# Attention, soft MoE and maxout on one core: loading q and k as pairs of tokens

## The chip, the cores and the metric

The kernel runs on one core of a Trainium2 chip. Five engines work side by side: TensorE (PE, with its weight loads as PEld), VectorE (DVE), ScalarE (ACT), GpSimd (POOL) and SyncE (SP), which issues the DMAs. The metric is the device time of one execution in microseconds.

## The reference

Three stages follow one another, all in float32:

```
scores = scale * q_c @ k_c^T          # 64-token chunks, 8 batches x 8 heads, 9 chunks, head size 64
attn = exp(scores - max) ; attn /= sum + 1e-9
out = attn @ v_c                      # -> x [4608, 512]

logits = x @ phi                      # soft MoE: 8 experts x 4 slots
slot_input = softmax over tokens(logits)^T @ x
h = relu(slot_input[e] @ w1[e]) ; slot_out[e] = h @ w2[e]
x = softmax over slots(logits) @ slot_out

h = max(x @ w1, x @ w2, x @ w3)       # maxout, 512 -> 768 -> 512
y = h @ w_out                         # these four weights arrive as float64
```

## The kernel before

The 4608 tokens are cut into 18 units of 256 tokens; an **item** is one unit and four of the eight heads, so there are 36 items, 0 to 35. The kernel has three stages: the attention loop over items (which also computes the logits, the running softmax over tokens and the slot sums, and decodes the float64 maxout weights to float32), the eight experts, and the maxout with the output.

The loop is pipelined by hand. In iteration i each name in `ORDER` emits one step for its item, and the instructions of every engine run in the order in which they were emitted. The steps that the change and the prediction touch, with their lines before the change:

- `ld` (L431 to L443): the loads on SP's queue: q and k of item i+3 (`load_qk`, L153), V (`load_v`, L144), one piece of float64 weight `r` (`load_raw`, L409), and now and then a 1 MB chunk `w` of expert weights (`load_chunk`, L114), of which `NPRE` = 13 are loaded inside the loop into memory that the attention does not use. 32 chunks are needed in all; the others are loaded as the attention's memory comes free, from line 572 on, and then as the experts use up the ring.
- `Tk`, `Tq` (L171): transposes of raw k and q of item i+1 on PE; `ke`, `qe` (L182, L178): their copies from PSUM to SBUF on ACT.
- `S` (L193): 32 matmul records of 64x64 scores of item i; `mx`, `sub` (L203, L208) on DVE; `exp` (L214) on ACT in the next iteration.
- `PT` (L222), `PTe` (L227), `PV` (L240): transpose of the exponentials, copy, product with V for item i-1.
- `rd`, `rec`, `nrm` (L250, L254, L260): normalisation on DVE for item i-2; `XT`, `XTe` (L275, L280): transpose of its result.
- `da` on ACT (L416), `d0`, `d1`, `d2` on DVE (L421, L423, L427): decoding of one piece `r`, in iterations 1 to 31; pieces have 256 columns (18) or 384 (12).
- every fourth iteration: `st` (L307 to L313, statistics of the logits), `ex` and `ss`, `eT`, `sm` and `sa` (L351 and L360, slot sums), `l0` and `l1` (L297).

A raw q or k tile has two buffers, `r` two, V two. One tile of q or k is loaded with tokens on the partitions: every token of a head is one 256-byte piece in memory (64 floats), 1024 such pieces for q and as many for k and for V in an iteration.

Of the kernel before, what the change touches and what calls it, by code (L numbers as in the profile page):

```python
# [8 lines left out]
F32 = mybir.dt.float32  # L9
# [3 lines left out]
ALU = mybir.AluOpType  # L13
# [5 lines left out]
def kernel(  # L19
# [32 lines left out]
    NPRE = 13  # L52
# [10 lines left out]
        "exp ex rd rec nrm ss d0 Tk Tq ke qe ld PT XT eT d1 PTe XTe eTe d2 S da sm sa l0 l1 mx sub PV st"  # L63
# [15 lines left out]
    ones1 = const.tile([1, 1], F32, name="ones1")  # L79
    wm_p = tc.alloc_tile_pool(name="wm_p", bufs=1, side="left")  # L80
    wm = wm_p.tile([128, 3, KM, DF], F32, name="wm")

    NV = 2
# [43 lines left out]
    raw_p = p1.enter_context(tc.tile_pool(name="raw", bufs=2, side="right"))  # L127
    r64_p = tc.alloc_tile_pool(name="r64", bufs=2, side="right")
# [24 lines left out]
    def load_qk(i):  # L153
        u, hh = divmod(i, 2)
        for src, nm in ((k, "kr"), (q, "qr")):
            t = raw_p.tile([128, 2, 4, D], F32, tag=nm, name=nm)
            for cp in range(2):
                for off, n, b, s in runs(u * UNIT + 128 * cp, 128):
                    nc.sync.dma_start(
                        out=t[off:off + n, cp], in_=src[b, 4 * hh:4 * hh + 4, s:s + n, :].rearrange("h p d -> p h d")  # L160
                    )
            raw[nm, i] = t

    qT, kT, tq = {}, {}, {}

    def emit_T(i, nm):
        src = raw.pop((nm, i))
        ps = ps_t.tile([128, 2, 2, 128], F32, tag="t", name="ps" + nm)
        for a in range(2):
            for cp in range(2):  # L170
                nc.tensor.transpose(  # L171
                    ps[:, a, cp, :], src[:, cp, 2 * a:2 * a + 2, :].rearrange("p e d -> p (e d)"), ident
                )
        tq[nm, i] = ps

    def emit_qevac(i):
        qT[i] = q_p.tile([128, 2, 2, 128], F32, tag="qT", name="qT")
        nc.scalar.copy(out=qT[i], in_=tq.pop(("qr", i)))  # L178

    def emit_kevac(i):  # L180
        kT[i] = k_p.tile([128, 2, 2, 128], F32, tag="kT", name="kT")
        nc.scalar.copy(out=kT[i], in_=tq.pop(("kr", i)))  # L182
# [3 lines left out]
    def emit_S(i):  # L186
        ps = ps_s.tile([128, 2, 512], F32, tag="s", name="pss")[:, :, 0:256].rearrange("p e (a c k) -> p e a c k", a=2, c=2)
        qt, kt = qT.pop(i), kT.pop(i)
        for a in range(2):
            for c2 in range(2):  # L190
                for e in range(2):
                    for cp in range(2):
                        nc.tensor.matmul(  # L193
                            ps[64 * cp:64 * cp + 64, e, a, c2, :],
                            lhsT=qt[64 * e:64 * e + 64, a, cp, 64 * c2:64 * c2 + 64],
                            rhs=kt[64 * e:64 * e + 64, a, cp, 64 * c2:64 * c2 + 64],
                            start=True, stop=True, tile_position=(64 * e, 64 * cp),
                        )
        s_ps[i] = ps.rearrange("p e a c k -> p e (a c) k")
# [231 lines left out]
    def loads_for(i):  # L431
        if i + 3 < NI:
            load_qk(i + 3)
        if i % 2 == 1 and i > 1 and (i + 1) // 2 < NU:
            load_v((i + 1) // 2)
# [7 lines left out]
    if True:  # L443
        make_identity(nc, ident)
        for t in vt:
            nc.gpsimd.memset(t[:, :, :, D:D + 1], 1.0)
# [3 lines left out]
        nc.sync.dma_start(out=phi_sb, in_=phi.rearrange("(k p) s -> p k s", p=128))  # L450
        emit_T(0, "kr")
        emit_T(0, "qr")
        emit_kevac(0)
        emit_qevac(0)
# [14 lines left out]
        def dstep(part):  # L469
# [11 lines left out]
            "ke": item(emit_kevac, 1), "qe": item(emit_qevac, 1), "ld": loads_for,  # L481
# [486 lines left out]
```

## Time and profile before

| | us |
|---|---|
| median of 3 runs (491.02 to 494.27) | 493.99 |
| the profiled execution | 488.15 |
| its span, first to last instruction | 486.3 |
| PE busy | 413.4 (85%) |
| DVE busy | 262.9 (54%) |
| ACT busy | 205.9 (42%) |
| POOL busy | 83.5 (17%) |

The span falls in three parts: the attention loop and its end up to about 234 us, the experts up to about 277 us, the maxout to the end. PE's share is high mainly because of the last part. A share of busy time over the whole span says little here; the stages are read apart, by stretches of the trace.

### The profile page before, as it was taken

To read this page: it belongs to the slowest core of one execution; us is meant where nothing else is said; L and a number is where in the kernel's file an instruction comes from. 1 tells how busy PE (TensorE), PEld (TensorE's weight loads), DVE (VectorE), ACT (ScalarE), POOL (GpSimd) and SP (SyncE) were. 2 spreads that over 40 slices of the span, in tenths; PEclk is the share of its full clock that TensorE was granted. 3 is DMA by queue.
4 is the path that set the end of the run, shared out by engine and by line. 5 is a ranking of instruction groups with operands and counts; after the bars stand their busy time and mean duration, and the time that the engine had idled before them with its cause. 6 is when DMAs were issued, how large, how long until landed. Compare 5 with 4: busy or idle time off the path is not lost.

```text
span 486.3 us, 11395 instructions
## 1 busy us (share of the span) xinstructions
PE 413.4 (85%) x4641; PEld 310.9 (64%) x4641; DVE 262.9 (54%) x580; ACT 205.9 (42%) x437; POOL 83.5 (17%) x77
## 2 busy tenths in 40 slices
PE   4869687786786787776899879999999999999996
PEld 3657564565564566654333548788888888888885
DVE  1367675575666666464373599743444444444430
ACT  3456564454464454553010565633433343334320
POOL 0000000000000000000000048643433334333330
PEclk9697988889889878799999988999999999999999
DMA  8999999999999999977899900111111111111111
GB/s 180 197 208 291 265 249 252 220 274 254 252 246 275 219 248 255 250 220 274 299 405 411 410 21 1 61 48 44 66 44 43 48 62 44 43 65 44 56 53 65
DMA packets 138020, 84.70 MB, mean 174 GB/s; under 512 B 115952, under 2 KB 116976, under 8 KB 137968
## 3 DMA queue, kind: packets, MB, share of 16 engines
q1 hardware_dynamic: 137968, 83.97, 61.3%
q8 instruction: 37, 0.61, 0.5%
q14 instruction: 15, 0.12, 0.1%
HBM read 74.51 MB, written 9.44 MB: 173 GB/s over the span
## 4 chain that ended last, share of the span: by engine, by line
PE 61%; DMA 19%; DVE 8%; ACT 6%; SPq 3%; issue 2%; ACTq 0%; DVEq 0%
PE ops L823 31%; DMA r<-in_moe_w_dram 18%; PE h L786 8%; PE pss L193 3%; PE psx L275 3%; PE pst L222 3%; ACT sx L214 2%; PE hps L597 2%; PE so L628 2%; SPq L147 2%; PE pso L240 2%; PE pskr L171 2%; PE lg L297 1%; DMA kr<-in_k_dram 1%; PE psqr L171 1%
## 5 line engine op out<-in xcount | busy, mean ns | idle before, releaser
L823 PE MATMUL ops<-wo,hhi 128*128 128x512 f32 x432 | 137.1, 399 | 0.0
L823 PEld LDWEIGHTS ops<-wo,hhi 128*128 128x128 f32 x432 | 81.3, 190 | 18.5
L802 POOL TENSOR_TENSOR hlo<-a,hhi 128x512 fp32r<-128x512 f32 (+1 forms) x60 | 72.5, 1210 | 108.8 <-ACT hhi L799 104.8
L823 PE MATMUL ops<-wo,hlo 128*128 128x512 f32 x216 | 85.9, 398 | 0.0
L795 DVE TENSOR_TENSOR a<-h,a 128x512 f32<-128x512 f32 (+1 forms) x60 | 38.2, 636 | 84.1 <-ACT a L791 83.8
L791 ACT COPY a<-h 128x512 f32<-128x512 f32 (+1 forms) x60 | 32.7, 545 | 95.0 <-PE h L786 94.5
L222 PE MATMUL pst<-ident,sx 128*128 128x128 f32 x144 | 26.5, 313 | 45.4 <-ACT sx L214 45.3
L222 PEld LDWEIGHTS pst<-ident,sx 128*128 128x128 f32 x144 | 18.1, 158 | 51.6 <-ACT sx L214 51.5
L203 DVE TENSOR_REDUCE mx<-pss 128x8 f32<-128x512 f32 x36 | 24.8, 690 | 42.6 <-PE pss L193 42.5
L823 PEld LDWEIGHTS ops<-wo,hlo 128*128 128x128 f32 x216 | 41.0, 190 | 10.2
L796 DVE TENSOR_TENSOR a<-h,a 128x512 f32<-128x512 f32 (+1 forms) x60 | 38.3, 638 | 6.2
L416 ACT ACTIVATE wm<-r 128x256 f32<-128x256 f32 (+1 forms) x30 | 14.4, 480 | 62.5 <-DMA r<-in_moe_w_dram 62.5
L574 POOL MEMSET hz<- 128x256 f32 x2 | 0.6, 311 | 231.4 <-PE slp L351 231.4
L799 ACT CAST hhi<-a 128x512 fp32r<-128x512 f32 (+1 forms) x60 | 34.7, 581 | 9.5 <-DVE a L796 9.5
L171 PE MATMUL pskr<-ident,kr 128*128 128x128 f32 x144 | 28.2, 317 | 7.5 <-DMA kr<-in_k_dram 7.4
L786 PE MATMUL h<-cstt,ast 128*128 128x512 f32 (+1 forms) x120 | 32.7, 385 | 0.3 <-DVE a L796 0.3
L240 PEld LDWEIGHTS pso<-vt,pT 64*64 64x64 f32 x1152 | 24.7, 159 | 11.8 <-issue 6.2
L214 ACT ACTIVATE sx<-sx 128x512 f32<-128x512 f32 x36 | 22.4, 622 | 22.6 <-DVE sx L208 22.6
L193 PE MATMUL pss<-kT,qT 64*64 64x64 f32 x1152 | 30.9, 257 | 1.1 <-issue 1.1
L193 PEld LDWEIGHTS pss<-kT,qT 64*64 64x64 f32 x1152 | 25.2, 163 | 9.1 <-issue 8.8
L240 PE MATMUL pso<-vt,pT 64*64 64x65 f32 x1152 | 29.4, 249 | 0.9 <-issue 0.6
L275 PE MATMUL psx<-ident,x 128*128 128x128 f32 x144 | 26.7, 316 | 3.0 <-DVE x L260 1.7
(127 smaller groups left out, 559.4 us busy)
## 6 DMA issues: line engine op xcount, KB each, us to landing
w<-in_moe_w_dram SPq DMA_DIRECT2D x31, 1024.0 KB, 7.1
out_dram<-ob SPq DMA_DIRECT2D x36, 256.0 KB, 2.0
kr<-in_k_dram SPq DMA_DIRECT2D x64, 128.0 KB, 4.7
qr<-in_q_dram SPq DMA_DIRECT2D x64, 128.0 KB, 4.6
vt<-in_v_dram SPq DMA_DIRECT2D x32, 256.0 KB, 5.0
r<-in_moe_w_dram SPq DMA_DIRECT2D x18, 256.0 KB, 4.5
r<-in_moe_w_dram SPq DMA_DIRECT2D x12, 384.0 KB, 5.3
wr<-in_moe_w_out_dram SPq DMA_DIRECT2D x3, 1024.0 KB, 12.6
```

Source lines behind the costliest of these rows:

```text
L171: nc.tensor.transpose(ps[:, a, cp, :], src[:, cp, 2 * a:2 * a + 2, :].rearrange("p e d -> p (e d)"), ident)
L193: nc.tensor.matmul(ps[64 * cp:64 * cp + 64, e, a, c2, :], lhsT=qt[64 * e:64 * e + 64, a, cp, 64 * c2:64 * c2 + 64], rhs=kt[64 * e:64 * e + ...
L222: nc.tensor.transpose(ps[:, n, :], t[:, n, :], ident)
L240: nc.tensor.matmul(ps[64 * cp:64 * cp + 64, c2, 65 * h:65 * h + 65], lhsT=t[64 * c2:64 * c2 + 64, 2 * e + a, 64 * cp:64 * cp + 64], rhs=vt ...
L275: nc.tensor.transpose(ps[:, a, c2, :], xs[u][:, c2, f0:f0 + 128], ident)
L786: nc.tensor.matmul(p, lhsT=a_st[t][:, i, f0:f0 + 128], rhs=cst(t0, n), start=True, stop=True)
L791: nc.scalar.copy(out=h_a[b, f], in_=h_ps[b, f][0])
L795: nc.vector.tensor_tensor(out=a, in0=ps[1], in1=a, op=ALU.max)
L796: nc.vector.tensor_tensor(out=a, in0=ps[2], in1=a, op=ALU.max)
L799: nc.scalar.copy(out=h_t[b][0][:, f, :], in_=h_a[b, f])
L802: nc.gpsimd.tensor_tensor(out=h_t[b][1][:, f, :], in0=h_a.pop((b, f)), in1=h_t[b][0][:, f, :].bitcast(F32), op=ALU.subtract)
L823: nc.tensor.matmul(ps, lhsT=a[:, f, 128 * t:128 * t + 128], rhs=wo_h[f // 2][:, f % 2, w, :], start=(f == 0 and n == 0), stop=(f == FB - 1 ...
```

## The change

Two neighbouring tokens of q and k are loaded together: partition p of a tile now holds tokens 2p and 2p+1 of the unit, 128 floats that lie side by side in memory, and a tile is loaded by one DMA rather than by two. The transposes (four per tile, as before) now give, for one head, the even tokens on partitions 0 to 63 and the odd ones on 64 to 127. The scores still need 64x64 blocks with the head on its own half of the partitions and tokens in order, so the halves are put back: k by four ACT copies of 64x256 straight from PSUM, with every second column written (`pairs`); q by one ACT copy into a new tile `qs` (one buffer) and then four GpSimd multiplications by one, 64x256 each, from `qs` to `qT` (new step `qp`). Raw q, k and `r` get three buffers instead of two, V three instead of two, and `NPRE` goes from 13 to 11. `ORDER` is written anew: `ld` comes first, `Tq` before `Tk`, `PTe` before `ke`, and `d2` after `sub`.

```
@@ -49,7 +49,7 @@
     NRING = 10
-    NPRE = 13
+    NPRE = 11
     DW = DF // 2
@@ -60,7 +60,7 @@
     ORDER = (
-        "exp ex rd rec nrm ss d0 Tk Tq ke qe ld PT XT eT d1 PTe XTe eTe d2 S da sm sa l0 l1 mx sub PV st"
+        "ld exp ex rd rec nrm ss Tq Tk qe qp PT d0 d1 XT eT PTe ke XTe eTe S mx sub sm sa l0 l1 da d2 PV st"
     )
@@ -77,10 +77,11 @@
     ones1 = const.tile([1, 1], F32, name="ones1")
+    ones4 = const.tile([128, 1, 1], F32, name="ones4")
     wm_p = tc.alloc_tile_pool(name="wm_p", bufs=1, side="left")
...
 
-    NV = 2
+    NV = 3
     rings = [tc.alloc_tile_pool(name="ring", bufs=NRING, side="left")]
@@ -124,8 +125,9 @@
     k_p = p1.enter_context(tc.tile_pool(name="kp", bufs=2, side="right"))
-    raw_p = p1.enter_context(tc.tile_pool(name="raw", bufs=2, side="right"))
-    r64_p = tc.alloc_tile_pool(name="r64", bufs=2, side="right")
+    qs_p = p1.enter_context(tc.tile_pool(name="qsp", bufs=1, side="right"))
+    raw_p = p1.enter_context(tc.tile_pool(name="raw", bufs=3, side="right"))
+    r64_p = tc.alloc_tile_pool(name="r64", bufs=3, side="right")
     ps_t = p1.enter_context(tc.tile_pool(name="ps_t", bufs=3, space=PSUM))
@@ -152,34 +154,48 @@
         u, hh = divmod(i, 2)
-        for src, nm in ((k, "kr"), (q, "qr")):
-            t = raw_p.tile([128, 2, 4, D], F32, tag=nm, name=nm)
-            for cp in range(2):
-                for off, n, b, s in runs(u * UNIT + 128 * cp, 128):
-                    nc.sync.dma_start(
-                        out=t[off:off + n, cp], in_=src[b, 4 * hh:4 * hh + 4, s:s + n, :].rearrange("h p d -> p h d")
-                    )
+        for src, nm in ((q, "qr"), (k, "kr")):
+            t = raw_p.tile([128, 4, 2, D], F32, tag=nm, name=nm)
+            for off, n, b, s in runs(u * UNIT, UNIT):
+                nc.sync.dma_start(
+                    out=t[off // 2:(off + n) // 2],
+                    in_=src[b, 4 * hh:4 * hh + 4, s:s + n, :].rearrange("h (p r) d -> p h r d", r=2),
+                )
             raw[nm, i] = t
 
-    qT, kT, tq = {}, {}, {}
+    qT, kT, qs, tq = {}, {}, {}, {}
 
...
         for a in range(2):
-            for cp in range(2):
-                nc.tensor.transpose(
-                    ps[:, a, cp, :], src[:, cp, 2 * a:2 * a + 2, :].rearrange("p e d -> p (e d)"), ident
-                )
+            for e in range(2):
+                nc.tensor.transpose(ps[:, a, e, :], src[:, 2 * a + e].rearrange("p r d -> p (r d)"), ident)
         tq[nm, i] = ps
 
+    def pairs(t, e, r):
+        return t[64 * e:64 * e + 64].rearrange("p a (g r) -> p a g r", r=2)[:, :, :, r]
+
     def emit_qevac(i):
-        qT[i] = q_p.tile([128, 2, 2, 128], F32, tag="qT", name="qT")
-        nc.scalar.copy(out=qT[i], in_=tq.pop(("qr", i)))
+        qs[i] = qs_p.tile([128, 2, 2, 128], F32, tag="qs", name="qs")
+        nc.scalar.copy(out=qs[i], in_=tq.pop(("qr", i)))
+
+    def emit_qpair(i):
+        qT[i] = q_p.tile([128, 2, UNIT], F32, tag="qT", name="qT")
+        src = qs.pop(i)
+        for e in range(2):
+            for r in range(2):
+                nc.gpsimd.tensor_tensor(
+                    out=pairs(qT[i], e, r), in0=src[64 * r:64 * r + 64, :, e, :],
+                    in1=ones4[64 * r:64 * r + 64].to_broadcast([64, 2, 128]), op=ALU.mult,
+                )
 
     def emit_kevac(i):
-        kT[i] = k_p.tile([128, 2, 2, 128], F32, tag="kT", name="kT")
-        nc.scalar.copy(out=kT[i], in_=tq.pop(("kr", i)))
+        kT[i] = k_p.tile([128, 2, UNIT], F32, tag="kT", name="kT")
+        src = tq.pop(("kr", i))
+        for e in range(2):
+            for r in range(2):
+                nc.scalar.copy(out=pairs(kT[i], e, r), in_=src[64 * r:64 * r + 64, :, e, :])
 
@@ -192,8 +208,8 @@
                             ps[64 * cp:64 * cp + 64, e, a, c2, :],
-                            lhsT=qt[64 * e:64 * e + 64, a, cp, 64 * c2:64 * c2 + 64],
-                            rhs=kt[64 * e:64 * e + 64, a, cp, 64 * c2:64 * c2 + 64],
+                            lhsT=qt[64 * e:64 * e + 64, a, 64 * (2 * cp + c2):64 * (2 * cp + c2) + 64],
+                            rhs=kt[64 * e:64 * e + 64, a, 64 * (2 * cp + c2):64 * (2 * cp + c2) + 64],
                             start=True, stop=True, tile_position=(64 * e, 64 * cp),
@@ -431,8 +447,8 @@
             load_qk(i + 3)
-        if i % 2 == 1 and i > 1 and (i + 1) // 2 < NU:
-            load_v((i + 1) // 2)
+        if i % 2 == 1 and (i + 3) // 2 < NU:
+            load_v((i + 3) // 2)
         if i < len(dec):
@@ -442,16 +458,18 @@
         make_identity(nc, ident)
+        nc.gpsimd.memset(ones4, 1.0)
         for t in vt:
...
         nc.sync.dma_start(out=phi_sb, in_=phi.rearrange("(k p) s -> p k s", p=128))
+        emit_T(0, "qr")
         emit_T(0, "kr")
-        emit_T(0, "qr")
+        emit_qevac(0)
+        emit_qpair(0)
         emit_kevac(0)
-        emit_qevac(0)
         load_qk(2)
@@ -478,7 +496,7 @@
             "Tk": item(lambda i: emit_T(i, "kr"), 1), "Tq": item(lambda i: emit_T(i, "qr"), 1),
-            "ke": item(emit_kevac, 1), "qe": item(emit_qevac, 1), "ld": loads_for,
+            "ke": item(emit_kevac, 1), "qe": item(emit_qevac, 1), "qp": item(emit_qpair, 1), "ld": loads_for,
             "S": item(emit_S, 0), "mx": item(emit_max, 0), "sub": item(emit_sub, 0), "exp": item(emit_exp, -1),
```

What moves on the queues, at three places of the loop (`w` is a chunk of expert weights, `vt` V, `r` a piece of float64 weight; a number behind a name is a buffer).

SP's queue, two iterations early in the loop, before:

```order
L147 DMA vt_120<-in_v_dram 64x8x64 x2
L147 DMA vt_120<-in_v_dram 128x8x64
L412 DMA r_397<-in_moe_w_dram 128x768
L159 DMA kr<-in_k_dram 128x4x64 x2
L159 DMA qr<-in_q_dram 128x4x64 x2
L412 DMA r_480<-in_moe_w_dram 128x768
L114 DMA w<-in_moe_w_dram 128x2x1024
```

and after the change:

```order
L149 DMA vt_124<-in_v_dram 128x8x64 x2
L428 DMA r_404<-in_moe_w_dram 128x768
L160 DMA qr<-in_q_dram 128x4x128
L160 DMA kr<-in_k_dram 128x4x128
L428 DMA r_492<-in_moe_w_dram 128x768
L115 DMA w<-in_moe_w_dram 128x2x1024
```

A row of q or k in memory is now 128 floats long instead of 64, with half as many of them; the order on this queue stays, but all of it is issued at the head of the iteration.

DVE, from one subtraction past the next (L208 before, L224 after), where slot sums (`acc`) fall, before:

```order
L208 TENSOR_TENSOR sx<-pss,mx 128x512
L250 TENSOR_SCALAR rd<-pso 128x8
L254 RECIPROCAL rd<-rd 128x8
L260 TENSOR_TENSOR x<-pso,rd 128x2x256
L421 TENSOR_SCALAR wm<-wm 128x256
L423 SCALAR_TENSOR_TENSOR wm<-r_659,wm 128x256
L427 SCALAR_TENSOR_TENSOR wm<-r_659,wm 128x256
L364 COPY acc<-slp 128x512
L203 TENSOR_REDUCE mx<-pss 128x8
```

and after:

```order
L224 TENSOR_TENSOR sx<-pss,mx 128x512
L443 SCALAR_TENSOR_TENSOR wm<-r_588,wm 128x256
L266 TENSOR_SCALAR rd<-pso 128x8
L270 RECIPROCAL rd<-rd 128x8
L276 TENSOR_TENSOR x<-pso,rd 128x2x256
L437 TENSOR_SCALAR wm<-wm 128x256
L439 SCALAR_TENSOR_TENSOR wm<-r_687,wm 128x256
L219 TENSOR_REDUCE mx<-pss 128x8
L224 TENSOR_TENSOR sx<-pss,mx 128x512
L380 COPY acc<-slp 128x512
L443 SCALAR_TENSOR_TENSOR wm<-r_687,wm 128x256
```

The third decode step (L427, now L443) now stands between the subtraction and the normalisation of the next iteration, and so does the slot sum, which stood ahead of the maximum.

ACT, one iteration before:

```order
L214 ACTIVATE sx<-sx 128x512
L182 COPY kT<-pskr 128x512
L178 COPY qT<-psqr 128x512
L227 COPY pT<-pst 128x512
L280 COPY xT<-psx 128x512
L416 ACTIVATE wm<-r_480 128x384
```

and after:

```order
L230 ACTIVATE sx<-sx 128x512
L181 COPY qs<-psqr 128x512
L243 COPY pT<-pst 128x512
L198 COPY kT<-pskr 64x256 x4
L296 COPY xT<-psx 128x512
L432 ACTIVATE wm<-r_492 128x384
```

Three more copies stand on ACT, and `qs` goes on to the four GpSimd instructions of line 188, of which there are 144 in the program; in the attention loop GpSimd had no work before.

## Rows read from the trace of the kernel before

**Rows 1.** The page, 40 slices: DMA busy share in tenths.
```profile
DMA  8999999999999999977899900111111111111111
```
**Rows 2.** The page, all DMA packets of the span by size.
```profile
DMA packets 138020, 84.70 MB, mean 174 GB/s; under 512 B 115952, under 2 KB 116976, under 8 KB 137968
```
**Rows 3.** Stretches: busy us per engine (records), granted clock, DMA share, GB/s.
```profile
25.00:200.00 175.00, 130.52 (x2550) 101.55 (x2553) 113.32 (x281) 91.35 (x200) 0.00 (x0) 0.87 1.03 250
...
240.00:260.00 20.00, 18.59 (x234) 7.55 (x226) 10.68 (x31) 1.57 (x3) 0.00 (x0) 1.00 1.03 407
...
270.00:275.00 5.00, 4.17 (x50) 1.99 (x42) 2.47 (x10) 1.24 (x4) 0.00 (x0) 1.00 1.07 407
```
**Rows 4.** Waits: engine, line, waited for, total us, times, longest.
```profile
ACT wm L416 <- DMA r<-in_moe_w_dram: 62.5, 24, 5.0
```
**Rows 5.** Score matmuls of L193: ns min/median/max, first and last start us.
```profile
L193 PE MATMUL pss<-kT,qT x1152: 218/218/367, 8.4 to 219.3; 64*64 64x64 f32 x192
```
**Rows 6.** Timeline, one iteration without a wait on DMA: start us, us, instruction.
```profile
26.67 0.69 PE L193 MATMUL pss<-kT,qT 64*64 64x64 f32 x32
...
27.44 0.69 DVE L203 TENSOR_REDUCE mx<-pss 128x8 f32<-128x512 f32 x1 [0.94 <-PE pss L193]
...
28.16 0.69 DVE L208 TENSOR_TENSOR sx<-pss,mx 128x512 f32<-128x512 f32 x1
...
28.89 0.63 ACT L214 ACTIVATE sx<-sx 128x512 f32<-128x512 f32 x1 [0.73 <-DVE sx L208]
...
29.19 0.69 DVE L260 TENSOR_TENSOR x<-pso,rd 128x512 f32<-128x512 f32 x1
...
29.57 0.66 PE L222 MATMUL pst<-ident,sx 128*128 128x128 f32 x4 [0.71 <-ACT sx L214]
...
30.06 0.64 PE L275 MATMUL psx<-ident,x 128*128 128x128 f32 x4
...
30.63 0.69 PE L193 MATMUL pss<-kT,qT 64*64 64x64 f32 x32
```
**Rows 7.** DVE by form, 25 to 200 us: count, busy us, mean ns.
```profile
L427 DVE SCALAR_TENSOR_TENSOR wm<-r,wm 128x256 int32<-128x256 int32 x17 | 7.2, 425 | 0.6
...
L421 DVE TENSOR_SCALAR wm<-wm 128x256 int32<-128x256 int32 x17 | 4.9, 286 | 4.4 <-ACT wm L416 4.4
...
L360 DVE SCALAR_TENSOR_TENSOR acc<-acc,nm,slp 128x512 f32<-128x512 f32 x5 | 3.7, 748 | 9.5 <-PE slp L351 9.5
```
**Rows 8.** ACT by form, 25 to 200 us.
```profile
L416 ACT ACTIVATE wm<-r 128x256 f32<-128x256 f32 x16 | 6.9, 434 | 33.6 <-DMA r<-in_moe_w_dram 33.6
```
**Rows 9.** GpSimd by form, whole span: count, busy us, mean ns.
```profile
L802 POOL TENSOR_TENSOR hlo<-a,hhi 128x512 fp32r<-128x512 f32 x48 | 62.2, 1297 | 90.6 <-ACT hhi L799 90.3
L802 POOL TENSOR_TENSOR hlo<-a,hhi 128x256 fp32r<-128x256 f32 x12 | 10.3, 864 | 18.1 <-ACT hhi L799 14.5 <-DVE ast L900 3.6
```
**Rows 10.** Timeline past 282 us: decode on DVE beside GpSimd.
```profile
282.39 5.50 POOL L768 TENSOR_TENSOR wo<-tmp,wo 128x512 fp32r<-128x512 f32 x3 [49.02 <-ACT wo L765]
...
282.97 0.68 DVE L423 SCALAR_TENSOR_TENSOR tmp<-wr,tmp 128x512 int32<-128x512 int32 x1
...
283.90 1.44 DVE L427 SCALAR_TENSOR_TENSOR tmp<-wr,tmp 128x512 int32<-128x512 int32 x1
...
285.60 1.16 DVE L421 TENSOR_SCALAR tmp<-tmp 128x512 int32<-128x512 int32 x1
...
286.79 1.65 DVE L423 SCALAR_TENSOR_TENSOR tmp<-wr,tmp 128x512 int32<-128x512 int32 x1
```
**Rows 11.** Timeline, end of the loop: scores of items 34 and 35.
```profile
213.92 0.69 PE L193 MATMUL pss<-kT,qT 64*64 64x64 f32 x32
...
218.85 0.69 PE L193 MATMUL pss<-kT,qT 64*64 64x64 f32 x32
```
**Rows 12.** The last chunk's two DMAs (L112): issue time, us to landing.
```profile
L112 SPq DMA_DIRECT2D w<-in_moe_w_dram x2: 2420/3450/4479, 258.3 to 260.8; - x2
...
DMA to landing us min/median/max: 13.5/14.1/14.6
```

More of the change, by code (lines that the diff above doesn't have):

```diff
@@ L169, in emit_T, with emit_qevac @@
         for a in range(2):
-            for cp in range(2):
-                nc.tensor.transpose(
-                    ps[:, a, cp, :], src[:, cp, 2 * a:2 * a + 2, :].rearrange("p e d -> p (e d)"), ident
-                )
-        tq[nm, i] = ps
-    def emit_qevac(i):
-        qT[i] = q_p.tile([128, 2, 2, 128], F32, tag="qT", name="qT")
-        nc.scalar.copy(out=qT[i], in_=tq.pop(("qr", i)))
+            for e in range(2):
+                nc.tensor.transpose(ps[:, a, e, :], src[:, 2 * a + e].rearrange("p r d -> p (r d)"), ident)
+        tq[nm, i] = ps
+    def pairs(t, e, r):
+        return t[64 * e:64 * e + 64].rearrange("p a (g r) -> p a g r", r=2)[:, :, :, r]
+    def emit_qevac(i):
+        qs[i] = qs_p.tile([128, 2, 2, 128], F32, tag="qs", name="qs")
[8 more added lines that the diff above has]
+                    in1=ones4[64 * r:64 * r + 64].to_broadcast([64, 2, 128]), op=ALU.mult,
+                )
     def emit_kevac(i):
-        kT[i] = k_p.tile([128, 2, 2, 128], F32, tag="kT", name="kT")
-        nc.scalar.copy(out=kT[i], in_=tq.pop(("kr", i)))
+        kT[i] = k_p.tile([128, 2, UNIT], F32, tag="kT", name="kT")
[3 more added lines that the diff above has]
+                nc.scalar.copy(out=pairs(kT[i], e, r), in_=src[64 * r:64 * r + 64, :, e, :])
     s_ps, sx, mxs = {}, {}, {}
```

## The prediction

> **What bounds the kernel now.** I read the page's slices first: the DMA engines are busy in nine tenths or more of nearly every slice of the first two hundred microseconds, and hardly at all after the experts [rows 1]. Then the stretches: from 25 to 200 us the DMA share is 1.03 at only 250 GB/s, while ACT is busy 91 of 175 us and DVE 113; in the experts the same share moves 407 GB/s [rows 3]. So the loop keeps the DMA engines full at 0.6 of the rate that they reach elsewhere. The packets say why: 115952 of 138020 are under 512 bytes [rows 2], and they are q, k and V. The waits agree: ACT's decode step waits 62.5 us for `r` [rows 4], and all that follows on ACT stands behind it. From the first score matmul at 8.4 us to item 35 at 218.85 us [rows 5, 11] an item takes (218.85 - 8.4)/35 = 6.0 us. An iteration that waits for no data takes 30.63 - 26.67 = 3.96 us [rows 6]. The loop is DMA-bound, with up to 2 us per iteration to win.
>
> **DMA, price of a packet.** The stretch from 25 to 200 us holds 175/6.0 = 29 items. Engine time: 175 x 16 x 1.03 = 2884 us. Bytes: 43.75 MB, of which q, k and V are 29 x 3072 x 256 B = 22.8 MB. The other 20.9 MB move at 407 GB/s / (16 x 1.03) = 24.7 B/ns [rows 3] and take 848 us. This leaves 2036 us for 89,100 pieces: 22.9 ns each. A 512-byte piece has no row. Its lower bound is the full rate, 20.7 ns; the upper one twice 22.9 = 45.8 ns. The nearest row speaks for the lower one: the last chunk moves in 1 KB pieces; it is issued from 258.3 us on and lands about 14 us later [rows 12], and 270 to 275 us still shows 407 GB/s [rows 3]. Had every piece a fixed cost that explains 22.9 ns (13.6 ns plus 0.036 ns a byte), 1 KB pieces would show some 330 GB/s. I take 21.5 ns.
>
> An iteration's q and k then cost 1024 x 21.5 instead of 2048 x 22.9: 24.9 us of engine time less, or 24.9/(16 x 1.03) = 1.5 us. Two chunks fewer in the loop are 2 x 1.05 MB/407 GB/s = 5.2 us, 0.16 per iteration. DMA per iteration: 6.0 - 1.5 - 0.16 = 4.35 us; 5.85 with the upper bound.
>
> **What is late next.** The chain of an iteration is scores, maximum, subtraction, exponential, transpose, transpose of x, scores: 0.77 + 0.72 + 0.73 + 0.68 + 0.49 + 0.57 = 3.96 us [rows 6]. The transpose of x also needs the normalisation, which ended at 29.88, just before it started at 30.06. The new order puts the third decode step, 0.43 us [rows 7], between subtraction and normalisation. That moves the normalisation to 30.31 and the chain to 4.28. GpSimd can add to it (next part). A 384-column piece (12 of 30) adds about 0.13 us to that step (half as many columns again), 0.05 on the mean.
>
> Every fourth iteration the slot sum (0.75 us [rows 7]) now also lies between subtraction and normalisation; the statistics lay there already, and an iteration with them, the exponentials and one more transpose takes 218.85 - 213.92 = 4.93, 0.97 more than the plain one [rows 6, 11]. Together (0.75 + 0.97)/4 = 0.43 per iteration.
>
> **GpSimd and the decode steps.** Four GpSimd instructions of 64x256 per iteration have no row. The nearest is its 128x256 subtraction, 0.86 us [rows 9], with two inputs too; I take that. Bounds: from 0.43 us, half of it for half the partitions, to 1.30 us, the row of 128x512, if writing every second column costs as the whole width. Beside them the three DVE decode steps slow down, as later in the trace: L423 takes 0.68 us alone, and 1.65 beside GpSimd; L427 takes 1.44, L421 1.16, and three GpSimd instructions 5.50 instead of 3 x 1.30 = 3.9 [rows 9, 10]. So they wait for each other; a step lost 0.76 to 0.97 us beside a 1.30 us instruction, and should lose up to half of it, 0.47, beside one of 0.86.
>
> Stepping through an iteration from the exponential (0): q's copy 0.51 to 1.10; GpSimd from 1.17, four instructions. The first decode step (ready at 1.5) waits to about 1.9, the second ends at 2.6, and the maximum, due at 3.0, is not delayed. GpSimd's second instruction is pushed by 0.4, and the fourth ends at 5.0. The third decode step, at 4.3 after the subtraction, meets the fourth instruction and waits up to 0.47; this pushes the normalisation, in some iterations and not in others. Half of it: +0.24. Mean iteration: 4.28 + 0.05 + 0.43 + 0.24 = 5.0 us; with 0.1 for a partial wait ahead of the maximum (a fifth of 0.47), **5.1 us**. This is above DMA's 4.35, so the loop is no longer DMA-bound.
>
> The single `qs` tile closes another ring: copy 0.59, four times 0.86, 0.4 lost to decode, 0.2 for hand-over: 4.6 us, inside 5.1. ACT gains three instructions net: 4 x 0.43 [rows 8] less 0.57 = 1.15 us, and 91.35/29 + 1.15 = 4.3 us [rows 3]; covered as long as the iteration is longer than that.
>
> The Trainium skill's page "SBUF — State Buffer", section "Who interferes with whom", says that DVE and GpSimd share one port pair under an exclusive lock, and that the loser blocks for the whole instruction. Rows 10 agree that they block each other; by the full rule each of three steps loses up to 0.86, which is the first rival below.
>
> **SP's queue and buffers.** `ld` moves to the head of the iteration and each tile has three buffers: the tile that a load overwrites was freed in the iteration before, so I expect SP to wait for little, and `r` to be issued nearly two iterations ahead of its use. Half the q and k DMAs go. I cost this at nothing; 5.1 us over 4.35 of DMA covers it.
>
> **Sum for the loop.** First scores at 8.4 as now: GpSimd's four instructions (3.44) come on top of q's path, but q and k arrive as earlier DMAs. Items 1 and 2 follow at the `qs` ring without decode, 4.2 us each. Then 29 items at 5.1, then four without decode and data waits: 2 x 3.96 + 4.93 + 4.7 = 17.6. Item 35: 8.4 + 8.4 + 147.9 + 17.6 = 182.3 instead of 218.85: **-36.5 us**.
>
> **The experts.** Two more chunks are left to load after the loop, 5.2 us of DMA. DMA is busy there to the end, and the last chunk lands at about 274 to 275 us [rows 12], so little hides them; some idle DMA time at the loop's end may. Between 0 and 5.2; I take **+3**. The maxout is untouched.
>
> Profiled time: 488.15 - 36.5 + 3 = 454.7. The median of the runs shown, 493.99, is 1.2% above that execution; carried over: **460 us**.
>
> **The rivals.** A difference under 1% can't be told from no change here.
>
> 1. *The port holds for whole instructions.* The first two decode steps then wait for one instruction each, and the maximum starts at 3.6 instead of 3.0 after the exponential: 5.7 us per item, 29 x 0.6 = 17 more, **478 us**. For it: the 1.65 in rows 10. Against it: the losses there (0.76 to 0.97) are less than the 1.30 of an instruction.
> 2. *GpSimd becomes the bound.* The `qs` ring is 1.16 + 4P (0.59 + 0.4 + 0.17). At P = 1.25 it is 6.2 us and the loop as long as before; at 1.30, 6.4 us: item 35 at 8.4 + 2 x 6.0 + 29 x 6.4 + 17.6 = 223.6, with +3 some 8 us slower: **502 us**. For it: no row shows a strided GpSimd write. Against it: 0.86 for as many columns in twice the partitions.
> 3. *The pieces are no cheaper.* If a 512-byte piece costs 46 ns, the loads do not do what the change says, and the loop stays at 5.9: **494 us**. Against it: rows 3 and 12. The Trainium skill's page "DMA: Bandwidth & Descriptors", section "Specifications", puts the line rate at 512 bytes and more; no run here shows 512 itself.
> 4. *The decode wait vanishes and the group steps hide* in the slack of the neighbours: 4.6 us per item, 29 x 0.5 = 15 less, **445 us**.
>
> **The numbers.** Forecast 0.56 (450 to 471), port 0.15, GpSimd bound 0.10, no cheaper 0.07, hidden 0.12. The range 446 to 484 takes in the forecast, the port case and half of the hidden one; some 0.2 is left out. Faster by over 1% (under 489): 0.56 + 0.15 + 0.12 = 0.83. Within 1%: 0.07. Slower: 0.10.
>
> **What would show it.** DMA share in the loop well under 1, with packets under 512 bytes down by 73,700; ACT's wait for `r` near nothing; scores 5.1 us apart; GpSimd instructions near 0.86 us; decode steps that take longer than 0.43; the experts up to 5 us longer. ACT's copy of q waiting for GpSimd would show rival 2; DMA still full in the loop, rival 3. The forecast fails first if GpSimd's price is over 1.1 us.

## The result and the profile after

| | before | after |
|---|---|---|
| median | 493.33 us (4 runs) | 474.37 us (4 runs, 471.40 to 476.31) |
| the profiled execution | 488.15 us | 471.4 us |
| its span | 486.3 us | 469.6 us |
| scores of the loop, first to last start | 8.4 to 219.3 us | 8.4 to 203.2 us |
| per item, that stretch over 35 | 6.03 us | 5.57 us |
| end of the scores to the first output matmul | 72.8 us | 73.1 us |

The changed kernel takes 0.9617 of the time before (95% interval 0.9553 to 0.9681): faster, but by 19 us and not by the 34 that were forecast. The span is 16.7 us shorter, the loop 16.1, and the experts are as long as before. So what there is to explain lies in the loop.

The page of the changed kernel, DMA busy share by slices and packets of the span:

```profile
DMA  8999999999999999888999600111111111111111
DMA packets 100134, 84.71 MB, mean 180 GB/s; under 512 B 41200, under 2 KB 79088, under 8 KB 100080
```

Packets under 512 bytes fell by 74,752, as they should [rows 2], but the first row looks as it did before [rows 1]: the DMA engines are still busy in nine tenths or more of every slice of the loop but the first and the last two. The prediction had named this as the sign of its third rival. The stretch agrees (the changed kernel by stretches: length, busy us and records of PE, PEld, DVE, ACT, POOL, granted clock, DMA share, GB/s):

```profile
25.00:175.00 150.00, 116.09 (x2426) 88.49 (x2424) 113.58 (x262) 114.25 (x266) 69.39 (x108) 0.94 1.05 261
25.00:200.00 175.00, 136.34 (x2871) 104.11 (x2869) 128.92 (x299) 133.44 (x310) 81.87 (x128) 0.94 1.03 263
```

From 25 to 200 us a share of 1.03 at 263 GB/s stands against 1.03 at 250 [rows 3]: hardly more bytes per microsecond. The changed kernel's waits (engine, line, what was waited for: total us, times, longest):

```profile
POOL qT L188 <- ACT qs L181: 99.3, 36, 9.0
...
ACT wm L432 <- DMA r<-in_moe_w_dram: 28.4, 15, 7.4
```

The decode still waits for `r`, 28.4 us where it was 62.5 [rows 4], and GpSimd stands idle for 99.3 us until its input is copied: it is not the bound. The scores of the changed kernel [rows 5], shortest, median and longest in ns, first and last start in us:

```profile
L209 PE MATMUL pss<-kT,qT x1152: 212/218/368, 8.4 to 203.2; 64*64 64x64 f32 x192
```

Last, what the joining does to DVE. The changed kernel by form, 25 to 200 us (count, busy us, mean ns, idle time before):

```profile
L188 POOL TENSOR_TENSOR qT<-qs,ones 64x256 f32<-64x256 f32 x128 | 81.9, 640 | 96.6 <-ACT qs L181 90.5
L198 ACT COPY kT<-pskr 64x256 f32<-64x256 f32 x128 | 50.9, 398 | 1.1
...
L439 DVE SCALAR_TENSOR_TENSOR wm<-r,wm 128x256 int32<-128x256 int32 x16 | 11.5, 718 | 0.6
...
L443 DVE SCALAR_TENSOR_TENSOR wm<-r,wm 128x256 int32<-128x256 int32 x17 | 7.1, 417 | 0.0
...
L437 DVE TENSOR_SCALAR wm<-wm 128x256 int32<-128x256 int32 x16 | 7.0, 439 | 0.0
```

A GpSimd instruction takes 0.64 us, less than the 0.86 taken. Beside it the first decode step takes 439 ns instead of 286 [rows 7] and the second 718; the third, moved behind the subtraction, takes 417, as it did before (425 [rows 7]).

### The profile page after: what moved, and what is told of

Its sections match the earlier page's. It is cut to its first block, busy times and chain, and to the rows that moved or that the text cites. A ratio compares the mean times of both kernels' runs of the same rounds, so it can differ in the third digit from the quotient of the medians.

```text
span 469.6 us, 11628 instructions
## 1 busy us (share of the span) xinstructions
PE 400.9 (85%) x4641; PEld 298.9 (64%) x4641; DVE 269.8 (57%) x580; ACT 243.8 (52%) x545; POOL 175.3 (37%) x223
## 4 chain that ended last, share of the span: by engine, by line
PE 55%; DMA 20%; DVE 10%; ACT 8%; issue 3%; SPq 2%; ACTq 0%; DVEq 0%
PE ops L841 32%; DMA r<-in_moe_w_dram 16%; PE h L804 8%; PE pst L238 2%; DMA wr<-in_moe_w_out_dram 2%; ACT sx L230 2%; PE pss L209 2%; ACT kT L198 2%; PE psx L291 2%; PE hps L615 2%; PE so L646 2%; DVE sx L224 1%; DVE mx L219 1%; ACT pT L243 1%; SPq L149 1%
## 5 line engine op out<-in xcount | busy, mean ns | idle before, releaser
L188 POOL TENSOR_TENSOR qT<-qs,ones 64x256 f32<-64x256 f32 x144 | 91.6, 636 | 106.2 <-ACT qs L181 99.3
L841 PEld LDWEIGHTS ops<-wo,hhi 128*128 128x128 f32 x432 | 80.9, 189 | 18.7
L198 ACT COPY kT<-pskr 64x256 f32<-64x256 f32 x144 | 57.1, 397 | 1.5 <-PE pskr L173 0.3
L238 PE MATMUL pst<-ident,sx 128*128 128x128 f32 x144 | 25.0, 299 | 35.5 <-ACT sx L230 35.2
L238 PEld LDWEIGHTS pst<-ident,sx 128*128 128x128 f32 x144 | 16.6, 149 | 42.4 <-ACT sx L230 42.4
L173 PE MATMUL psqr<-ident,qr 128*128 128x128 f32 x144 | 25.1, 300 | 7.5 <-DMA qr<-in_q_dram 7.5
L291 PE MATMUL psx<-ident,x 128*128 128x128 f32 x144 | 24.9, 300 | 6.8 <-DVE x L276 5.3
L256 PEld LDWEIGHTS pso<-vt,pT 64*64 64x64 f32 x1152 | 21.8, 140 | 12.7 <-issue 7.8
L432 ACT ACTIVATE wm<-r 128x256 f32<-128x256 f32 (+1 forms) x30 | 14.6, 486 | 28.4 <-DMA r<-in_moe_w_dram 28.4
L256 PE MATMUL pso<-vt,pT 64*64 64x65 f32 x1152 | 26.7, 228 | 2.5 <-issue 2.2
L209 PE MATMUL pss<-kT,qT 64*64 64x64 f32 x1152 | 28.2, 240 | 0.5 <-issue 0.5
L786 POOL TENSOR_TENSOR wo<-tmp,wo 128x512 fp32r<-128x512 f32 x6 | 9.8, 1655 | 49.5 <-ACT wo L783 49.3
```

Of the source, the lines that this page charges most:

```text
L188: nc.gpsimd.tensor_tensor(out=pairs(qT[i], e, r), in0=src[64 * r:64 * r + 64, :, e, :], in1=ones4[64 * r:64 * r + 64].to_broadcast([64, 2, ...
L198: nc.scalar.copy(out=pairs(kT[i], e, r), in_=src[64 * r:64 * r + 64, :, e, :])
L209: nc.tensor.matmul(ps[64 * cp:64 * cp + 64, e, a, c2, :], lhsT=qt[64 * e:64 * e + 64, a, 64 * (2 * cp + c2):64 * (2 * cp + c2) + 64], rhs= ...
L238: nc.tensor.transpose(ps[:, n, :], t[:, n, :], ident)
L256: nc.tensor.matmul(ps[64 * cp:64 * cp + 64, c2, 65 * h:65 * h + 65], lhsT=t[64 * c2:64 * c2 + 64, 2 * e + a, 64 * cp:64 * cp + 64], rhs=vt ...
L291: nc.tensor.transpose(ps[:, a, c2, :], xs[u][:, c2, f0:f0 + 128], ident)
```

## The experiments

The table gives each run's median, its ratio to the kernel before on the same chip, and the time per item as above. Two kernels were profiled once and not timed in rounds; they have sections of their own.

| run | what it changes | us | ratio (95%) | us per item |
|---|---|---|---|---|
| the change | | 474.37 | 0.9617 (0.9553 to 0.9681) | 5.57 |
| e2_old_path | no pairs, the rest kept | 491.57 | 0.9932 (0.9892 to 0.9971) | 6.02 |
| e3_q256 | pairs in 256-byte pieces | 506.94 | 1.0222 (1.0152 to 1.0291) | 6.52 |
| e4_no_v | V left out | 455.95 | 0.9183 (0.9103 to 0.9263) | 5.00 |
| e5_r_first | `r` ahead of q, k and V | 475.11 | 0.9572 (0.9528 to 0.9615) | 5.56 |
| e6_r_early | `r` an iteration earlier | 474.73 | 0.9563 (0.9522 to 0.9605) | 5.57 |
| e7_no_v_no_pool | no V, no GpSimd | 454.13 | 0.9165 (0.9125 to 0.9206) | 4.90 |
| e8_r_early_d2 | third decode step back | 475.89 | 0.9605 (0.9574 to 0.9635) | 5.60 |
| e10_v_pitch | V's rows 80 floats apart | 478.03 | 0.9633 (0.9531 to 0.9734) | 5.71 |
| e11_deep | q, k four items ahead | 476.37 | 0.9622 (0.9550 to 0.9694) | 5.62 |
| e12_no_pool | no GpSimd | 473.11 | 0.9518 (0.9435 to 0.9602) | 5.46 |

### What a piece costs (e1_pieces)

A kernel that only loads, eight tiles of a kind after another, each kind in pieces of another size:

```
for st in (q256, q512, q256p, q1k, vp(65), vp(64), vp(68), vp(72), vp(80), w2k):
    for n in range(8):
        st(n)
```

> This kernel computes nothing: it loads 2 MB per stage, eight loads of 256 KB, with a pause between stages, and stores zeros. Stages in order: q in 256-byte pieces; q in 512-byte pieces (token pairs); q in 256-byte pieces into the pair layout; q in 1 KB pieces; V in 256-byte pieces at a row pitch of 65, 64, 68, 72 and 80 floats; expert weights in 2 KB pieces. Theory A (a 512-byte piece is dearer than the prediction took, and V at its pitch of 65 floats dearer than q): engine time per piece about 18 ns for q at 256 bytes, 28 ns at 512, 30 ns or more for V at 65 and about 18 at 64. Theory B (the prediction's sizes): 23 ns at 256 bytes for q and V alike, 21.5 ns at 512, 42 at 1 KB.

Stretches of that kernel that lie inside one kind (length, DVE and POOL, clock, DMA share, GB/s): q in 256-byte pieces, the same laid out in pairs, V with its rows 65 floats apart, q in 512-byte pieces, q in 1 KB, and weights in 2 KB.

```profile
8.50:13.50 5.00, 0.00 (x0) 0.00 (x0) 1.00 0.98 219
41.00:47.00 6.00, 0.00 (x0) 0.00 (x0) 1.00 1.01 221
73.00:80.00 7.00, 0.00 (x0) 0.00 (x0) 1.00 1.38 222
25.00:29.00 4.00, 0.00 (x0) 0.00 (x0) 1.00 0.97 267
57.50:59.50 2.00, 0.00 (x0) 0.00 (x0) 1.00 0.98 335
158.00:162.00 4.00, 0.00 (x0) 0.00 (x0) 1.00 1.03 333
```

Twice the size brings 267/219 = 1.2 times the rate, not twice, and 1 KB brings 335, with no step at 512; 2 KB brings no more. Theory A was near for q (16 x 256/219 = 18.7 ns a piece, and 30.7 at 512 bytes) and wrong for V, whose pieces take 18.5 ns. These rates are rough: the stretches are short, outputs were stored between them, and inside the one of 512-byte pieces the rate goes from 181 GB/s (27 to 28 us, engines not full) to 331 (28 to 29 us). So I took the prices for the sum from e9_loads_alone instead.

The kernel before moves 1 KB pieces of weights faster. Its packets from 270 to 275 us, the stretch that the prediction went by:

```profile
DMA packets 1277, 2.03 MB, mean 407 GB/s; under 512 B 46, under 2 KB 993, under 8 KB 1277
```

993 - 46 = 947 of them, some half of the bytes, are the last chunk's 1 KB pieces. Why they go at 407 GB/s there, and those of q at 335 here, isn't shown.

### The other half of the change, and the pieces (e2_old_path, e3_q256)

e2_old_path keeps the new order, the buffers and `NPRE` = 11, and takes out the pairs (loads, transposes, copies and GpSimd as before). e3_q256 keeps everything and loads each half of a pair by a DMA of its own:

```
+                for r in range(2):
+                    nc.sync.dma_start(
+                        out=t[off // 2:(off + n) // 2, :, r, :],
+                        in_=src[...].rearrange("h (p r) d -> p h r d", r=2)[:, :, r, :],
+                    )
```

> The kernel before with the new buffers (three for raw q and k, r, V), the new order of steps and 11 chunks in the loop, but q and k loaded, transposed and copied as before: no pairs, no GpSimd. Theory A (what was won came from fewer pieces): DMA per item stays at 6.0 us less 0.16 for the chunks, so 488 us, -5. Theory C (what was won came from the earlier issue and the deeper buffers): close to the changed kernel, 474 to 478 us.

> The changed kernel with every q and k load cut into two DMAs of 256-byte pieces into the same layout; all else kept. Theory A: 2048 pieces of 18 ns instead of 1024 of 28 ns per item cost 8 us of engine time, 0.5 us per item, +18 us: 492 us. Theory C: no difference, 474 us. The prediction's size (21.5 against 22.9 ns) would give +1.5 us per item, +50 us.

The score rows of the two, e2_old_path first:

```profile
L193 PE MATMUL pss<-kT,qT x1152: 218/218/367, 8.7 to 219.4; 64*64 64x64 f32 x192
```

```profile
L210 PE MATMUL pss<-kT,qT x1152: 218/218/367, 8.8 to 237.0; 64*64 64x64 f32 x192
```

Buffers and order alone leave the loop where it was (6.02 and 6.03 us per item), although two chunks fewer are loaded in it. With pieces of 256 bytes the new path is slower than the kernel before by 1.5 to 2.9%, some 30 us above the change, between theory A and the prediction's size. So the gain comes from the larger pieces alone. e3_q256 also shows a cost of the path itself: it moves pieces of the size of e2_old_path's and needs 0.5 us more per item, at a DMA share of 0.92 over 25 to 200 us where e2_old_path has 0.98. It issues more DMAs than the change does, so this 0.5 isn't the path's price there.

### Transfers or chain (e4_no_v, e7_no_v_no_pool)

V is loaded for three units only and those are used for all (so PV multiplies other data); in e7_no_v_no_pool, besides, the copy of q's transposes writes `qT` directly and the halves stay apart.

```
-        if i % 2 == 1 and (i + 3) // 2 < NU:
-            load_v((i + 3) // 2)
+        if i == 1:
+            load_v(2)
```

> The changed kernel with V loaded for the first three units only; the other units use what lies in the three buffers, so the output is not the reference's. This takes a fifth of the loop's bytes and all of its V pieces off the DMA queue. Theory A (DMA still sets the loop, V about 33 ns a piece): DMA falls from 5.3 to 3.3 us per item and the loop goes to the compute chain; with the prediction's 5.1 us per item it is 458 us, with 4.6 us 441. Theory D (the loop already runs at the compute chain with GpSimd and the decode steps): 474 us, unchanged.

> The changed kernel without V past the third unit (as the run before this one) and without GpSimd's four instructions: the copy of q writes its tile directly, so its halves are not put in order and the output is not the reference's. Against the run without V (456 us, 4.99 us an item) this prices what GpSimd costs the decode steps on DVE and the chain. The prediction's terms (0.24 + 0.1 us an item) give -10 us: 446 us. A port that is held for whole instructions (0.6 more an item) would give -25 us: 431. No cost at all: 456.

Scores of e4_no_v, then of e7_no_v_no_pool:

```profile
L209 PE MATMUL pss<-kT,qT x1152: 218/218/367, 8.4 to 183.5; 64*64 64x64 f32 x192
```

```profile
L206 PE MATMUL pss<-kT,qT x1152: 213/218/366, 8.4 to 179.9; 64*64 64x64 f32 x192
```

With V's pieces gone (half of the changed kernel's pieces of q, k and V, a third of their bytes) and no instruction of the chain changed, the last item starts 1.2 us from where the prediction had it (182.3). So the chain was priced right, 5.00 us per item, and in the changed kernel it isn't the chain alone that sets the loop. Without GpSimd as well the loop is 3.6 us shorter in these two profiles, not 10, and the intervals of the two ratios overlap. The stretch of e4_no_v, in the columns used above, shows the DMA engines idle for once:

```profile
25.00:175.00 150.00, 126.43 (x2735) 96.06 (x2739) 131.71 (x292) 129.21 (x300) 78.72 (x123) 0.98 0.87 249
```

### Moving the wait (e5_r_first, e6_r_early, e8_r_early_d2)

`r` is what ACT waits for, so it might only be asked for too late. e5_r_first issues it ahead of q, k and V in `ld`; e6_r_early also gives it a fourth buffer and asks one iteration earlier; e8_r_early_d2 is that with the third decode step back ahead of the scores.

```
     def loads_for(i):
+        if i < len(dec):
+            load_raw(i)
         if i + 3 < NI:
             load_qk(i + 3)
...
-        if i < len(dec):
-            load_raw(i)
```

> The changed kernel with the load of the float64 piece r ahead of q, k and V in every iteration, nothing else. In the changed kernel ACT's decode step waits 28.4 us for r, and the loop is about the compute chain (4.99 us an item, as without V) plus that wait. Theory E (the wait is the place in the queue: r goes out last and is needed first, the DMA engines have room): the wait falls under 8 us and nothing takes its place, 452 to 460 us. Theory F (the wait is throughput, the DMA engines have no room): the wait moves to q, k or V, time within 1% of 474 us.

> As the one before, with a fourth buffer for r and each piece loaded one iteration earlier. Theory E: no wait for r is left, 450 to 458 us, at most 5 us better than with r first. Theory F: within 1% of 474 us, with waits on q and k instead.

> r one iteration early with four buffers, and the third decode step put back ahead of the maximum, as in the kernel before. The prediction put that step's new place at 0.32 us of chain an item plus 0.24 for the wait on GpSimd: if the loop runs at the chain, -9 to -16 us against the run with r early. If DVE is full or the maximum is then late by as much, no difference; if the DMA engines set the loop, no difference either.

The wait in e6_r_early:

```profile
PE psqr L173 <- DMA qr<-in_q_dram: 26.4, 15, 5.1
```

ACT no longer waits for `r`; instead PE waits 26.4 us for q (7.5 in the changed kernel), and the loop ends at 203.3 us as before. From 8 to 205 us all waits for loads together come to 27.6 us, where the changed kernel has 32.4. A wait that changes its place and nearly keeps its size belongs to the queue and not to the load that it stands at. The step put back gains nothing either.

### All loads alone (e9_loads_alone)

Eight phases of 20 items each; a phase loads what the loop loads and does nothing with it but touch a column on DVE, and a reduction on DVE behind the last touch marks its end.

```
    phase((qk_single, load_v(65), load_r, load_w(13)))
    phase((qk_pair, load_v(65), load_r, load_w(11)))
    phase((qk_pair, load_r, load_w(11)))
    phase((qk_single,))
    phase((qk_pair,))
    phase((load_v(65),))
    phase((load_r, load_w(11)))
    phase((qk_pair, load_v(80), load_r, load_w(11)))
```

> The loop's loads without the loop: nothing is computed, one element of each tile is read to free it, four buffers each. Eight phases of 20 items with a pause between them: the loads of the kernel before (q, k in 256-byte pieces, V, r, chunks at 13 in 36); those of the changed kernel (512-byte pieces, 11 in 36); these without V; q and k alone in 256-byte pieces; alone in 512; V alone; r and chunks alone; the changed kernel's with V at a row pitch of 80 floats. Theory F (the DMA engines set the changed loop): 5.8 to 6.0 us an item for the first phase, 5.3 to 5.5 for the second, near 4.4 without V; q and k alone 2.4 us an item at 256 bytes and 1.7 to 1.9 at 512 (the prediction's sizes would give 2.9 and 1.4). Theory G (DMA and compute hinder each other, loads alone would be faster): 5.0 for the first and 4.4 for the second phase, as the prediction had it.

The reductions that end the eight phases (start in us):

```profile
119.56 0.67 DVE L131 TENSOR_REDUCE gate<-gate 128x1 f32<-128x510 f32 x1
...
223.70 0.67 DVE L131 TENSOR_REDUCE gate<-gate 128x1 f32<-128x510 f32 x1
...
303.62 0.67 DVE L131 TENSOR_REDUCE gate<-gate 128x1 f32<-128x510 f32 x1
...
359.88 0.67 DVE L131 TENSOR_REDUCE gate<-gate 128x1 f32<-128x510 f32 x1
...
402.69 0.67 DVE L131 TENSOR_REDUCE gate<-gate 128x1 f32<-128x510 f32 x1
...
430.53 0.67 DVE L131 TENSOR_REDUCE gate<-gate 128x1 f32<-128x510 f32 x1
...
467.12 0.67 DVE L131 TENSOR_REDUCE gate<-gate 128x1 f32<-128x510 f32 x1
...
568.80 0.67 DVE L131 TENSOR_REDUCE gate<-gate 128x1 f32<-128x510 f32 x1
```

The first phase starts at 0.7 us and each other one 1.3 us behind the reduction ahead of it. Over 20 items, per item:

- the loads of before: (119.56 - 0.7)/20 = **5.94** us; the loop took 6.03
- the loads of after: (223.70 - 119.56 - 1.3)/20 = **5.14** us; the loop takes 5.57
- those without V: 3.93 us
- q and k in 256-byte pieces: 2.75 us; in 512-byte pieces: **2.07** us
- V: 1.33 us; `r` and chunks: 1.77 us
- the loads of after with V's rows 80 floats apart: 5.02 us

The parts add up: 2.07 + 1.33 + 1.77 = 5.17. The second phase comes out between the two theories (5.3 to 5.5, and 4.4). The larger pieces are worth 0.68 us per item, where the prediction had 1.5. A 512-byte piece takes 2.07 x 16/1024 = 32 ns of an engine, a 256-byte one 2.75 x 16/2048 = 21.5 (a phase's start and end included). Inside the fifth phase the engines are full from end to end, and a 512-byte piece takes 512 x 16/270 = 30 ns:

```profile
363.00:401.00 38.00, 5.69 (x37) 0.00 (x0) 1.00 1.18 270
```

The stretches of the first two phases (length, DVE and POOL, clock, DMA share, GB/s):

```profile
5.00:115.00 110.00, 11.23 (x73) 0.00 (x0) 1.00 1.03 250
125.00:219.00 94.00, 11.01 (x72) 0.00 (x0) 1.00 1.10 279
```

Alone the loads of before reach the loop's 250 GB/s [rows 3]; the new ones reach 279, of which the loop gets 261.

### V's rows (e10_v_pitch)

V's tile puts 64 floats into rows 65 floats apart. In e1_pieces its share of 1.38 stood out, so I tried 80:

```
-    vt = [v_p.tile([128, 2, H, D + 1], F32, name=f"vt{i}") for i in range(NV)]
+    vt = [v_p.tile([128, 2, H, 80], F32, name=f"vt{i}") for i in range(NV)]
```

> The changed kernel with V's rows in SBUF 80 floats apart instead of 65 (ones still in column 64), nothing else. In the run of pieces V moved at 222 GB/s at pitch 65, at 236 at pitch 80, 6% more. Theory F: V is a fifth of the bytes and costs about 1.2 us an item, so 0.07 us an item, -2.5 us: 472 us. If the loop isn't set by DMA: no change.

In the kernel no difference can be measured, and V alone costs per piece what q does (1.33 us for 1024, 2.75 for 2048). Loads alone do show one: 236 GB/s against 222 in e1_pieces, and 5.02 us per item against 5.14 in e9_loads_alone, one run of each. The loop doesn't pass it on.

### The last 0.4 us (e11_deep, e12_no_pool)

The loop needs 0.43 us per item more than its loads alone. Either the loads run out of room to run ahead, or work beside them slows them. e11_deep gives raw q and k a fourth buffer, asks for them four items ahead, and issues `r` first:

```
-    raw_p = p1.enter_context(tc.tile_pool(name="raw", bufs=3, side="right"))
+    raw_p = p1.enter_context(tc.tile_pool(name="raw", bufs=4, side="right"))
...
+        if i + 4 < NI:
+            load_qk(i + 4)
```

e12_no_pool takes GpSimd out as e7_no_v_no_pool does, and loads V:

```
-        for e in range(2):
+        for e in range(0):
```

> The changed kernel with r ahead of q, k and V in the load, a fourth buffer of raw q and k, and q and k asked for four items ahead instead of three; V, chunks and GpSimd as they are. With V left out the loop ran at 4.99 us an item (the chain), the loads alone at 5.14, and together they take 5.54. Theory C (the two are coupled: a load is issued only when a buffer is free and SP is not held, so the DMA engines stand idle now and then; one more buffer lets them run on): the loop falls toward 5.14 to 5.2 us an item, 0.34 to 0.4 x 35 = 12 to 14 us, 460 to 462 us, and the DMA share in 25:200 rises from 1.05 toward 1.10. Theory F (what is lost is lost in the DMA engines themselves, because SBUF and HBM have other work beside the loads; the look-ahead is enough): 472 to 476, loop end at 203, the waits moved again.

> The changed kernel without GpSimd's joining: the copy of q's transposes writes qT itself, so the two halves of q stay apart and the sums of q with its rows are not formed (output not the reference's); all loads, V too, stay. It prices GpSimd's four instructions of each item, with their effect on VectorE's decode steps and the wait of TensorE for qT, where the DMA engines set the time. The prediction's terms for these in the chain were 0.32 + 0.24 us an item, 20 us in 36 items, of which GpSimd alone some 10. Theory F (the DMA engines at 5.14 to 5.5 us an item set the loop): 0 to 4 us faster, 470 to 474 us. Theory P (VectorE beside GpSimd delays the decode, and so the item, whenever the loads come in time): 10 us or more, 464 or less.

The stretch in e11_deep, then in e12_no_pool (columns as for the changed kernel):

```profile
25.00:175.00 150.00, 112.26 (x2416) 84.63 (x2414) 113.24 (x262) 112.81 (x264) 67.60 (x107) 0.95 1.05 264
```

```profile
25.00:175.00 150.00, 117.94 (x2512) 90.67 (x2513) 105.18 (x265) 116.43 (x273) 0.00 (x0) 0.95 1.07 268
```

A fourth buffer brings nothing. Without GpSimd the loop ends at 199.8 us, 3.4 earlier in this one profile, and the ratio's interval overlaps that of the change. DVE's steps there are back at their old length (e12_no_pool by form):

```profile
L436 DVE SCALAR_TENSOR_TENSOR wm<-r,wm 128x256 int32<-128x256 int32 x17 | 7.2, 426 | 0.6
...
L434 DVE TENSOR_SCALAR wm<-wm 128x256 int32<-128x256 int32 x16 | 4.5, 283 | 0.0
```

So the delay of DVE beside GpSimd is real (718 against 426 ns), and GpSimd with all that hangs on it costs the loop about 0.1 us per item, as far as these two profiles tell. The rest of the 0.43, some 0.3, isn't settled. What is known: in the loop the DMA engines move 261/279 = 0.94 of their rate alone, at 0.95 of the share, so by the share most of it is time in which they are not busy. SP's queue offers a suspect (SP's own waits, 25 to 175 us; first the kernel before, its only line for V, then the largest for V in the changed kernel):

```profile
SPq L147 <- DMA w<-in_moe_w_dram: 0.4, 1, 0.4
```

```profile
SPq L149 <- PE pss L209: 6.5, 4, 3.0
SPq L149 <- PE pskr L173: 6.3, 3, 3.1
SPq L149 <- PE psx L291: 5.5, 2, 4.4
SPq L149 <- PE pso L256: 5.4, 2, 3.5
...
SPq L149 <- PE psqr L173: 4.9, 3, 2.3
SPq L149 <- PE pst L238: 4.7, 4, 1.8
```

Line 149 loads V. It overwrites a buffer whose last product is one of the last steps of the iteration before, and `ld` now stands at the head of the iteration; so SP stands there for 40 of 150 us (all lines for V), with everything behind it in the queue; the kernel before stood there for 0.4. On all its loads SP waits 72 us, where it waited 26. e2_old_path has the new order too: 23 us at V's load, a DMA share of 0.98 instead of 1.03, and no gain from its two chunks fewer. SP's waiting alone proves nothing: in e4_no_v it is 96 us in all, and the loop is faster. The other runs don't decide it: in e5_r_first and e11_deep SP stands at V's load for 34 and 31 us all the same, and e4_no_v takes away V's transfers and this stand together. A fourth V buffer, or V's load at the iteration's end, wasn't tried. Nor was the granted clock set apart, 0.94 in the changed loop and 0.98 in e4_no_v.

## Why the prediction came out as it did

- **What bounds the kernel before: right.** Its loads alone take 5.94 us per item, its loop 6.03.
- **The price of a piece: the step that failed.** "A 512-byte piece has no row ... I take 21.5 ns". It takes 30 to 32 (e9_loads_alone). The prediction had worked out the right answer, a fixed 13.6 ns plus 0.036 ns a byte, which gives 32 ns at 512 bytes, and dropped it because the last chunk's 1 KB pieces fell in 5 us at 407 GB/s [rows 3, 12]. That reading holds, as half of the bytes there are such pieces (e1_pieces); what failed is the step from 1 KB pieces of weights to 512-byte pieces of q and k. The price of a 256-byte piece was nearly right (21.5 against 22.9 ns), as was the rest (848/(29 x 16 x 1.03) - 0.16 = 1.61 us per item for `r` and 11 chunks by the prediction's numbers, 1.77 measured).
- **DMA per item: 5.14 us, not 4.35.** It did not fall under the chain but came out level with it. "The loop is no longer DMA-bound" was wrong, and so was the line on the wait for `r`: 28.4 us are left, and pushing it away from `r` puts it on q.
- **SP's queue: costed at nothing, without a run to show it.** "I expect SP to wait for little" was wrong: 72 of 150 us instead of 26, most of the increase at V's load. Whether this costs time is open.
- **The chain of 5.0 to 5.1 us: right, in part by luck.** It takes 5.00 where V is left out; over the whole loop the prediction had (182.3 - 8.4)/35 = 4.97. Its parts were less right. GpSimd's instruction takes 0.64 us, not 0.86, and its delays cost 3.4 to 3.6 us (e12_no_pool, e7_no_v_no_pool) instead of 0.34 x 29 = 10. Without them the prediction has (182.3 - 8.4 - 10)/35 = 4.7 us per item and e7_no_v_no_pool 4.90: two errors of some 0.2 us cancel. The row of 0.68 us that the prediction calls "alone" starts 0.58 us into GpSimd's stretch [rows 10]. What the moved decode step costs was not shown, since in the changed kernel the chain alone isn't what sets the time.
- **The loop as the longer of two numbers: too simple.** By 5.14 us the last item would start at 8.4 + 35 x 5.14 = 188 us. It starts at 203. Of the 20 us that the loop misses, 6 are the longer transfers and some 15 the 0.43 us per item by which the loop exceeds both, of which the runs explain a quarter at most. So the greater part of the miss has no shown cause. Where one of the two was far ahead it held twice (6.03 against 5.94 before, 5.00 where transfers need 3.93) and failed once: the loads of e3_q256 come to 2.75 + 1.33 + 1.77 = 5.85 us by their parts, and its loop takes 6.52.
- **The experts: +3 forecast, 0.3 in the profile of the change.** With `NPRE` = 11 and the old path the time from the last scores to the first output matmul is 75.5 us instead of 72.8 (e2_old_path), +2.7 as forecast; in the changed kernel it is 73.1. One profile doesn't settle it: the other runs with 11 chunks go from 72.8 (e12_no_pool) to 77.0 (e4_no_v, e6_r_early).
- **The sum.** Loop 20 us late, experts 2.7 and maxout 0.9 early, and the runs' median 0.6% above the profiled execution instead of 1.2%: 460 becomes 474.
- **The rivals.** The first (port, 478 us) lies nearest to the measured time and is wrong: without GpSimd next to nothing comes back. That 474 lies within 446 to 484 is owed to the room left for it, so that is luck. The second fell with 0.64 us. The third had the sign right (DMA still full) and the price too high: per byte the pieces are cheaper by a quarter, where it had nothing and the forecast half. The fourth fell: even without GpSimd's delays the chain takes 4.90 us, not 4.6.

The Trainium skill's page "DMA: Bandwidth & Descriptors", section "Specifications", puts the minimum for the line rate at 512 bytes. The runs disagree for loads into SBUF: 267 GB/s (e1_pieces) and 270 (e9_loads_alone) at 512 bytes, against 407 in the experts [rows 3].

The Trainium skill's page "SBUF — State Buffer", section "Who interferes with whom", calls the port pair that DVE and GpSimd share an exclusive lock. The lengthened steps (718 against 426 ns, 439 against 283) agree that there is a conflict; the mean loss of 0.16 to 0.29 us is less than half of a GpSimd instruction of 0.64 us.

## What to carry to other kernels

Price a piece size from two sizes that the trace shows, with a fixed part and a part per byte, before believing that doubling a piece halves its cost per byte; a kernel that issues only the loads gives the answer in one run. When transfers and compute come out as near to each other as here (5.14 and 5.00 us), expect the loop to take longer than either, as this one did, and put the forecast there; e3_q256 did so with the two further apart. A wait that moved from one load to the next without shrinking much lay in the queue here, and three reorderings of the loads won nothing back. Price what a new place in the program does to the queue that issues the loads: ahead of V's load it went from 0.4 to 40 us of waiting, and whether that cost time is still open here.

## What was not expected of the hardware

- In short stretches of a kernel that only loads, the DMA engines move 219, 267 and 335 GB/s at 256, 512 and 1024 bytes a piece, and no more at 2 KB (333).
- GpSimd with every second column written (64x256) takes 0.64 us, less than its dense 128x256 subtraction at 0.86 [rows 9].
- V's rows of 65 floats cost little more than rows of 64 or 80: 222, 228 and 236 GB/s in e1_pieces.
